# Linear attention with a soft mixture of experts on one core: the log magnitudes as two F32R parts, the key and query factors in one product, the turns found on ScalarE, and a new order of issue

## The chip, the core and the metric

The kernel runs on one core of a Trainium2 chip. The metric is the device time of one execution in microseconds, as the median of several runs. The engines are TensorE (PE, with its weight loads PEld), VectorE (DVE), ScalarE (ACT), GpSimd (POOL) and SyncE (SP), which issues all transfers here.

## The reference

Two parts follow each other. The first is a gated linear attention with complex decay, for 4 batches, 8 heads, 768 tokens and 48 channels:

```
scale = min(|a|, 0.999) / (|a| + 1e-6);  a = a * scale          # a = a_re + i a_im
for t in tokens:
    S = a[t][:, None] * S;  S.re += k[t] v[t]^T                 # 48 x 48 per head
    y[t] = q[t] . S.re
```

The second takes y as x of 3072 tokens by 384 channels and applies a soft mixture of 8 experts with 4 slots each: logits x @ phi, a softmax over all tokens that forms the 32 slots, two matrix products with a relu per expert, and a softmax over the slots that mixes their outputs into each token.

## The kernel before, in words

The tokens are cut into 24 blocks of 128 (six of each batch, g = 0 to 23), and three blocks make a unit u of 0 to 7. Tokens lie on the partitions; the 8 x 48 = 384 channels lie along a row. Instead of stepping through the tokens, each block is worked in polar form, with these steps (each a generator whose pieces are issued one at a time):

- `gates` (g in the order table; whole units, the first unit in two groups of 1 and 2 blocks): on ScalarE and VectorE, from the two parts of a, the tangent of the angle in `aat[:, 1]` and twice the log magnitude in `aat[:, 0]`. L642, L644, L646, L652 and L656 are on ScalarE; L648, L650, L654 and L658 on VectorE.
- `arctan` (t): the angle, L665 on ScalarE.
- `phase` (p, per block): L676 sums the angles along the tokens by a triangular product (`up`, in turns, since the triangle holds 1/2pi). VectorE rounds to whole turns by adding and subtracting a large constant (L679, tile `n`) and subtracts (L681, tile `f`); ScalarE takes sine (L686) and cosine (L691) into `cs`. L673 adds the block before's last turn to this block's first row.
- `expo` (e, per block): L702 sums the log magnitudes by another triangular product (`lp`, F32); L706 and L708 take its exponent with both signs into `ee`. One row of it goes to memory and comes back as the block's total decay (L711, L715).
- `mults` (m, per block): L723 multiplies `ee` with queries and keys; L732 then forms, for queries and for keys, the product with `cs`: two products of 768 columns into `hat0` and `hat1`. Block 0 does its part in two pieces (L728).
- `xpose` (x): four transposes per half of the heads and per side (L744, `tp`), copied by ScalarE (L747, `hT`).
- `score` (c): L752 (`sp`), masked by VectorE (L756, `scT`).
- `attend` (a): L777 and L779 into `yb`, copied by ScalarE as `yT` (L782).
- `delta` (D): the state's update, L790 (`db`), L795, L797 (`st`).
- `xform` (f), `logits` (l), `slots` (s), `shares` (q): the output turned back (`xp`, `xs`) and the running softmax sums of the experts' slots (`lg`, `mt`, `sip`, `lt`, `lct`).

After block 23 come `merge`, the experts (`hidden`, `turn`, `experts`) and the mixing (`combine0`, `combine1`) with the stores. Exponent and logarithm are in one table of ScalarE, sine and arctangent in another; L577 and L580 load them in turn, about once each per unit. `warm` (wu) issues a product whose result nobody reads.

What sets the order of the work is a long text, `ORDER`. Each name in it issues the next piece of that step, and `_InOrder` ties each instruction to the one before it on its engine. So the engines work in the order of this text, each at its own pace, and a wait holds up all that stands behind it on the same engine. The loads (la, lq, lv, w) are names in the same text and go to SP's queue.

Of the kernel before, what the change touches and what calls it, by code (L numbers as in the profile page):

```python
# [86 lines left out]
class _Moe:  # L87
# [227 lines left out]
    wu3 c5 g3 T2 p3 p3 p3 e4 a1 m4 p5 p5 m3 c4 la2 c5 D2 D2 a2 t3 m3 x14 x14 p4 m3 p5 p4 p4 p6 g3 p5 p5 x12 x12 a2 a2 p5 e5 g4
    D2 D3 D3 m4 m4 x16 x16 x15 x15 p6 D2 p6 x18 m5 p7 x13 x13 l0 p7 L3 x18 m5 m5 l0 p7 D3 g4 g4 f1 f1 x17 p8 x17 c6 e7 e7 e7 f2
    g4 c6 c7 f2 e6 e6 e6 x23 x23 x19 g4 g4 lq1 p8 e8 a3 c7 a3 l0 s0 e8 p8 g4 d1 q0 q0 e8 x20 w0 x19 x20 g4 D3 a3 T3 p6 p6 p8 c8
    c8 p8 g4 x21 x21 c9 c9 D4 D4 D4 x22 e6 x22 m6 p7 p7 a4 a4 D4 c10 c11 lv1 m6 x26 t4 p7 p9 m6 p9 c10 p8 p9 a4 x25 x24 s0 D5 D5
    e7 m7 e8 L4 a5 c11 a5 x25 x24 c12 x26 p10 m7 la3 g5 x28 m7 q0 s0 q0 p10 f3 c12 x27 a5 g5 d2 D5 a6 q0 g5 x28 D6 f3 p10 q0 g5
    x30 x30 x27 m8 g5 m8 x29 e9 e9 m8 e9 x31 x31 e10 e10 e9 l1 l1 e10 g5 c13 c13 x29 x34 x34 e11 c14 e11 lq2 e11 g5 p11 g5 c14  # L320
    q1 f4 f4 q1 q1 T4 D6 D6 x33 x35 x35 x32 x32 g5 p11 a6 a6 p11 p11 p9 p9 p9 c15 c15 s0 s0 s0 x33 p11 e10 m10 a7 a7 p10 c17 m9
    p10 t5 c16 a7 p11 D6 lv2 D7 D7 m9 x36 p10 q1 q1 p12 c16 la4 a8 c17 a8 g6 L5 e11 g6 g6 x38 x38 q1 e13 m9 p12 a8 x39 x39 lv3
    e12 D7 D8 D8 x36 e12 e12 x37 m10 x42 p13 m10 x37 g6 w1 l1 s1 x40 c18 x40 g6 x42 c19 D7 g6 x43 x41 e13 e13 d3 c18 a9 c19 a9
    a9 x41 m11 D8 D9 x43 m11 m11 e12 e14 e14 e14 g6 g6 f7 p13 p13 p14 x47 x47 lq3 m12 f7 T5 c21 c21 p12 c20 D9 p12 c20 p12 x45
    t6 x46 x46 x45 s1 p14 D8 f5 f5 x44 p14 x44 a10 a10 s1 l2 la5 p15 p15 m12 x50 D9 x50 e13 m12 p13 p13 p13 c22 e14 g6 x49 x48
    x49 x48 p14 p14 c22 p14 D10 D10 a10 l2 q2 c23 p15 D9 d4 p15 p16 p16 g7 p15 p15 q2 c23 x51 x51 m13 m13 f6 s1 f6 a11 a11 a11
# [756 lines left out]
```

## Time and profile before

| | |
|---|---|
| median of the runs shown | 300.86 us (299.57 to 302.11, 3 runs) |
| the profiled execution | 302.44 us |
| its span, first to last instruction | 300.6 us |
| busy: PE, PEld, DVE, ACT, POOL | 271.5, 214.2, 236.5, 213.5, 2.8 us |
| chain that ended last, by engine | PE 65%, DMA 12%, ACT 11%, DVE 7% |
| mean granted TensorE clock | 0.960 |

A row of the groups reads: line, engine, operation, output from inputs, shape and count, then the busy time in us and the mean of one in ns, then the idle time of that engine just before and what ended it. F32 products show two records each. In the rows of stretches the columns are the length, the busy time (and count) of PE, PEld, DVE, ACT and POOL, the granted TensorE clock (1.00 is full), the transfers' share and their rate. A row in order of time gives the start, the time taken and what was done; in brackets stands the idle time before it.

### The profile page before, as it was taken

What the parts mean: (1) busy time and instruction counts of PE and PEld (TensorE: products, weight loads), DVE (VectorE), ACT (ScalarE), POOL (GpSimd) and SP (SyncE); (2) the same over time, 40 slices, a digit from 0 to 9 for tenths busy, and PEclk for the clock granted to TensorE, in tenths of its full rate; (3) what the DMA queues carried; (4) which work ended last, traced back from release to release, by engine and by line L of the source; (5) the groups of instructions that cost most, each with busy time, mean ns of one, the idle gap of its engine ahead of it and who ended that gap; (6) DMA issues with size and microseconds to landing.
All of it is one profiled execution on the core that took longest, in us unless ns stands there. A gap on an engine that the chain in (4) does not pass through costs nothing.

```text
span 300.6 us, 6641 instructions
## 1 busy us (share of the span) xinstructions
PE 271.5 (90%) x2694; PEld 214.2 (71%) x2694; DVE 236.5 (79%) x453; ACT 213.5 (71%) x377; POOL 2.8 (1%) x7
## 2 busy tenths in 40 slices
PE   0649599989999999899999999999999999999990
PEld 0135488778888877888878887888898997336760
DVE  1468789899999999999998999998979565714350
...
GB/s 244 422 219 3 75 86 3 98 313 48 142 98 2 80 295 89 186 126 160 3 15 302 354 375 11 14 190 240 218 19 266 148 423 256 241 342 423 184 384 200
DMA packets 20788, 54.85 MB, mean 182 GB/s; under 512 B 11536, under 2 KB 13456, under 8 KB 16144
## 3 DMA queue, kind: packets, MB, share of 16 engines
...
q8 instruction: 23, 0.38, 0.6%
q14 instruction: 13, 0.11, 0.1%
...
## 4 chain that ended last, share of the span: by engine, by line
PE 65%; DMA 12%; ACT 11%; DVE 7%; issue 2%; SPq 0%; DVEq 0%; ACTq 0%
PE sp L752 12%; PE tp L744 11%; DMA aat<-in_aa_dram 8%; PE yb L777 6%; PE db L790 5%; DMA rows<-ee 5%; PE lp L702 4%; PE yb L779 4%; PE up L676 4%; PE hp L229 3%; PE op L259 3%; PE xp L802 3%; PE lg L109 2%; PE ep L277 2%; ACT gt L642 2%
## 5 line engine op out<-in xcount | busy, mean ns | idle before, releaser
L747 ACT COPY hT<-tp 96x512 f32<-96x512 f32 x96 | 53.5, 583 | 17.9 <-PE tp L744 17.8
L744 PE MATMUL tp<-cst,hat 128*96 128x128 f32 x384 | 57.2, 287 | 4.0 <-DVE hat L732 3.8
L744 PEld LDWEIGHTS tp<-cst,hat 128*96 128x96 f32 x384 | 45.0, 134 | 13.5 <-issue 5.8
L752 PE MATMUL sp<-hT,hT 96*128 96x128 f32 x384 | 51.6, 282 | 0.9 <-ACT hT L747 0.9
L752 PEld LDWEIGHTS sp<-hT,hT 96*128 96x128 f32 x384 | 47.2, 194 | 5.3 <-issue 2.5
L732 DVE TENSOR_TENSOR hat<-ee,cs 128x768 f32<-128x768 f32 x48 | 44.6, 951 | 2.3 <-PE tp L744 0.9
L777 PE MATMUL yb<-scT,vt 128*48 128x128 f32 x384 | 37.2, 280 | 3.5 <-DVE scT L756 3.5
L756 DVE TENSOR_TENSOR scT<-sp,cst 128x512 f32<-128x512 f32 x48 | 32.6, 684 | 3.7 <-PE sp L752 3.5
L790 PEld LDWEIGHTS db<-vt,hat 128*96 128x96 f32 x320 | 30.2, 165 | 4.2 <-issue 1.7
L790 PE MATMUL db<-vt,hat 128*96 128x48 f32 x320 | 30.8, 246 | 1.3 <-DVE st L795 1.3
L779 PE MATMUL yb<-hT,st 96*48 96x128 f32 x320 | 31.2, 272 | 0.0
L777 PEld LDWEIGHTS yb<-scT,vt 128*48 128x48 f32 x384 | 21.2, 123 | 11.2 <-issue 3.9
L723 DVE TENSOR_TENSOR ee<-ee,qkt 128x768 f32<-128x768 f32 x23 | 21.8, 951 | 4.8 <-DMA rows<-ee 3.3
L676 PE MATMUL up<-aat,cst 128*128 128x384 f32 x48 | 21.5, 532 | 3.2 <-ACT aat L665 2.9
L702 PE MATMUL lp<-aat,cst 128*128 128x384 f32 x48 | 21.5, 531 | 0.9 <-DVE aat L658 0.5
L779 PEld LDWEIGHTS yb<-hT,st 96*48 96x48 f32 x320 | 19.2, 123 | 0.0
L782 ACT COPY yT<-yb 128x512 f32<-128x512 f32 x24 | 14.0, 582 | 6.5 <-PE yb L779 6.5
L648 DVE TENSOR_TENSOR aat<-aat,gt 128x1152 f32<-128x1152 f32 (+2 forms) x9 | 11.0, 1219 | 8.8 <-ACT gt L646 8.8
L805 ACT COPY xs<-xp 128x384 f32<-128x384 f32 x24 | 11.3, 476 | 8.6 <-PE xp L802 8.6
L679 DVE TENSOR_SCALAR n<-up 128x384 f32<-128x384 f32 x24 | 13.2, 550 | 2.6 <-PE up L676 2.5
L802 PE MATMUL xp<-cst,yT 128*128 128x128 f32 x96 | 14.4, 274 | 0.4 <-DVE scT L756 0.4
L706 ACT ACTIVATE ee<-lp 128x384 f32<-128x384 f32 x24 | 11.8, 492 | 4.2 <-PE lp L702 4.0
...
## 6 DMA issues: line engine op xcount, KB each, us to landing
...
```

Source lines behind the costliest of these rows:

```text
L676: PE.matmul(out=up, lhsT=tri_u[par], rhs=ph, start=True, stop=True)
L702: PE.matmul(out=lp, lhsT=tri_l[par], rhs=aat[u][:, 0, j], start=True, stop=True)
L723: DVE.tensor_tensor(out=e, in0=e, in1=qkt[u][:, j], op=ALU.mult)
L732: DVE.tensor_tensor(out=x, in0=e[:, w].rearrange("p (h d) -> p h d", d=D).unsqueeze(2).broadcast_to([P, H, 2, D]), in1=cs[g], op=ALU.mult,)
L744: PE.transpose(out=tp[:, a, :], in_=hat[g][w][:, 4 * hh + a].rearrange("p c d -> p (c d)"), identity=ident)
L747: ACT.copy(out=hT[g, hh, w], in_=tp)
L752: PE.matmul(out=sp[:, a, :], lhsT=hT[g, hh, 1][:, a, :], rhs=hT[g, hh, 0][:, a, :], start=True, stop=True)
L756: DVE.tensor_tensor(out=t, in0=sp, in1=mask[g % 2].unsqueeze(1).broadcast_to([P, 4, P]), op=ALU.mult)
L777: PE.matmul(out=o, lhsT=vt[u][:, j, h, :], rhs=scT[g, hh][:, a, :], start=True, stop=first)
L779: PE.matmul(out=o, lhsT=st[g - 1][:, h, :], rhs=hT[g, hh, 0][:, a, :], start=False, stop=True)
L790: PE.matmul(out=db[:, h, :], lhsT=hat[g][1][:, h].rearrange("p c d -> p (c d)"), rhs=vt[u][:, j, h, :], start=True, stop=True)
L802: PE.transpose(out=xp[:, c].rearrange("p a d -> p (a d)"), in_=yT[g][:, c, :], identity=ident)
```

## The change

Five edits, and the order text written anew.

- `gates` ends with two more pieces: ScalarE copies the log magnitude into an F32R tile (its first part), and VectorE subtracts that from the full value into a second F32R tile. `expo` makes two F32R products of these in place of the F32 one, with F32R copies of the triangles (`tri_t`, one VectorE copy at the start).
- `phase` rounds on ScalarE: the large constant is the bias of a copy of `up`. VectorE subtracts constant and `up` in one instruction, which turns the sign of `f`; the scales of its users are turned too.
- `mults` makes one product of 1536 columns for queries and keys together, in a tile with two buffers (before, one of 768 for queries and two for keys). Block 0 is handled like the others.
- Fourteen warming products in place of four. They read a tile that GpSimd sets to zero, and so wait for no transfer.
- The scratch for dynamic transfers is set to 1024.

```diff
-BUF = dict(wx=7, wt=2, f=3, cs=4, ee=3, hat0=1, hat1=2, hT0=4, hT1=3, scT=2, st=2, xs=5, yT=5, we=4)
+BUF = dict(wx=7, wt=2, f=3, cs=4, ee=3, hat=2, hT0=4, hT1=3, scT=2, st=2, xs=5, yT=5, we=4)
 ORDER = """
-    i0 L0 g0 g0 g0 i6 i1 wu2 wu1 g0 g0 g0 g0 i3 g0 g0 i4 i2 g1 g1 e0 i8 g1 g1 la0 i7 e0 e0 wu0 lv0 T0 t0 g1 t1 e0 p0 p0 p0 p0 p0
+    wu13 wu2 L0 i0 g0 g0 wu12 g0 g0 i4 i3 i2 g1 wu6 g0 g0 wu9 i1 i5 g0 wu0 g1 tr0 g0 g0 g0 wu4 g0 g1 e0 wu10 e0 e0 wu8 T0 t0 g1
...
-    tri_l = [cst[:, C_TL : C_TL + P], cst[:, C_TL + P : C_MK]]
+    tri_t = cp.tile([P, 2 * P], F32R, name="tri_t")
+    tri_r = [tri_t[:, 0:P], tri_t[:, P : 2 * P]]
...
         DVE.scalar_tensor_tensor(out=ar, in0=ar, scalar=W_MAX, in1=t, op0=ALU.min, op1=ALU.subtract)
+        yield "g9"
+        if u not in parts:
+            parts[u] = [eo.tile([P, UB, HD], F32R, name=f"w{x}", bufs=1) for x in range(2)]
+        hi, lo = (w[:, j0:j1] for w in parts[u])
+        ACT.activation(out=hi, in_=ar, func=AF.Copy)
+        yield "g10"
+        DVE.tensor_tensor(out=lo, in0=ar, in1=hi.bitcast(F32), op=ALU.subtract)
...
-        DVE.tensor_scalar(out=n, in0=up, scalar1=MAGIC, scalar2=MAGIC, op0=ALU.add, op1=ALU.subtract)
+        ACT.activation(out=n, in_=up, func=AF.Identity, bias=kb[:, 4:5])
+        yield "p2b"
...
-        DVE.tensor_tensor(out=f, in0=up, in1=n, op=ALU.subtract)
+        DVE.scalar_tensor_tensor(out=f, in0=n, scalar=MAGIC, in1=up, op0=ALU.subtract, op1=ALU.subtract)
...
-        PE.matmul(out=lp, lhsT=tri_l[par], rhs=aat[u][:, 0, j], start=True, stop=True)
+        for x in range(2):
+            PE.matmul(out=lp, lhsT=tri_r[par], rhs=parts[u][x][:, j], start=x == 0, stop=x == 1)
...
-        for w in range(2):
-            if g == 0:
-                yield f"n{w}"
-                DVE.tensor_tensor(out=e[:, w], in0=e[:, w], in1=qkt[u][:, j, w], op=ALU.mult)
-            yield f"m{w}"
-            x = wk.tile([P, H, 2, D], F32, name=f"hat{w}", bufs=BUF[f"hat{w}"])
-            hat[g].append(x)
...
+        x = wk.tile([P, 2, H, 2, D], F32, name="hat", bufs=BUF["hat"])
+        hat[g] = [x[:, w] for w in range(2)]
+        sh = [P, 2, H, 2, D]
+        DVE.tensor_tensor(
+            out=x,
+            in0=e.rearrange("p w (h d) -> p w h d", d=D).unsqueeze(3).broadcast_to(sh),
+            in1=cs[g].unsqueeze(1).broadcast_to(sh),
+            op=ALU.mult,
+        )
...
+    blank = cp.tile([P, P], F32, name="blank")
+    POOL.memset(blank, 0.0)
...
-        PE.matmul(out=wp, lhsT=ident, rhs=cst[:, 0:512], start=True, stop=True)
-    for x in range(4):
+        PE.matmul(out=wp.rearrange("p (a c) -> p a c", a=4), lhsT=blank, rhs=blank.unsqueeze(1).broadcast_to([P, 4, P]), start=True, stop=True)
+    for x in range(14):
...
+    at("tr", lambda: DVE.tensor_copy(out=tri_t, in_=cst[:, C_TL:C_MK]) and None)
...
-    nc = _bacc.Bacc("TRN2", target_bir_lowering=False, num_devices=1)
+    nc = _bacc.Bacc("TRN2", target_bir_lowering=False, num_devices=1, dynamic_dma_scratch_size=1024)
```

Three places show what the new order text does. First TensorE's queue at the start, before (`wp` is a warming product, `hat` a block's factors):

```order
L904 MATMUL wp<-cst 128x512 x2
L702 MATMUL lp<-aat,cst 128x384
L904 MATMUL wp<-cst 128x512
L676 MATMUL up<-aat,cst 128x384
L744 MATMUL tp<-cst,hat_170 96x128 x8
```

and now:

```order
L913 MATMUL wp<-blank 128x512 x7
L713 MATMUL lp<-w_149,tri_t 128x384
L713 MATMUL lp<-w_150,tri_t 128x384
L913 MATMUL wp<-blank 128x512 x2
L685 MATMUL up<-aat,cst 128x384
L913 MATMUL wp<-blank 128x512
L685 MATMUL up<-aat,cst 128x384
L750 MATMUL tp<-cst,hat 96x128 x4
```

Seven warming products now stand ahead of the first `lp` pair, two between it and the first `up`, and the second block's `up` comes ahead of the first transposes. `w_149` is the first part, `w_150` the second.

Next ScalarE's queue at the start, before:

```order
L646 ACTIVATE gt<-aat 128x384
L652 ACTIVATE gt<-gt,kb 128x384
L656 ACTIVATE gt<-aat,kb 128x384
L642 ACTIVATE gt,amiss<-aat,kb 128x768
L644 ACTIVATE aat<-aat 128x768
L646 ACTIVATE gt<-aat 128x768
L706 ACTIVATE ee<-lp 128x384
```

and now:

```order
L648 ACTIVATE gt<-aat 128x384
L644 ACTIVATE gt,amiss<-aat,kb 128x768
L654 ACTIVATE gt<-gt,kb 128x384
L646 ACTIVATE aat<-aat 128x768
L658 ACTIVATE gt<-aat,kb 128x384
L665 ACTIVATE w_149<-aat 128x384
L648 ACTIVATE gt<-aat 128x768
L717 ACTIVATE ee<-lp 128x384
```

The passes of 768 columns (blocks 1 and 2) are now woven between those of block 0, and the first part (L665) stands ahead of the third of them.

Last SP's queue at the start, before:

```order
L617 DMA aat<-in_aa_dram 128x2x384
L596 DMA vt<-in_vv_dram 128x1152
L617 DMA cst<-in_consts_dram 128x640
L617 DMA aat<-in_aa_dram 128x2x384 x2
L617 DMA qkt<-in_qk_dram 128x768
```

and now:

```order
L619 DMA aat<-in_aa_dram 128x2x384 x3
L619 DMA qkt<-in_qk_dram 128x768
L619 DMA cst<-in_consts_dram 128x640
L619 DMA cst<-in_consts_dram 128x741
L590 DMA aat<-in_aa_dram 128x2304
```

All three blocks of `aat` come first; the constants, which the warming products no longer read, come after them and after the first queries and keys.

More of the change, by code (lines that the diff above doesn't have):

```diff
@@ L315 @@
[L315 to L326, printed above, removed]
@@ new lines @@
+    p5 p5 x13 x15 x15 g3 x10 la2 x10 p6 p6 p6 a1 x12 g3 p5 p5 p5 L3 c5 c5 D2 a2 a2 a2 p7 p7 p7 m5 g4 x12 g4 x14 x14 g4 D3 g3 D3
+    f0 f0 m4 p7 l0 l0 m5 l0 e6 e6 e6 x16 x16 lv1 c6 c6 d1 g4 f2 g4 f2 e7 e7 e7 e8 e8 e8 x17 x17 c7 c7 x21 x21 p8 g4 lq1 q0 D3 q0
+    q0 s0 D3 x20 x20 g4 x19 x19 p8 D4 p8 a3 a3 g4 x18 x18 T3 x22 w1 D4 e6 m6 e7 p8 p6 p6 p6 lq2 a3 la3 c8 q0 q0 x22 x23 g4 g4 c8
+    x23 t4 c10 p8 p8 p8 a4 p7 p7 c9 p7 m6 x24 D4 e8 x27 x27 g5 m7 d2 c9 x24 D5 D5 D4 m8 q0 p9 c10 s0 s0 a4 a4 p9 p9 f1 m7 f1 c11
@@ new lines @@
+    c11 x25 x25 L4 a5 a5 g5 x26 x26 c12 g5 p9 g4 e9 e9 e9 p10 f3 e9 f3 c13 a5 m8 c12 x31 g5 e10 e10 e10 c13 x29 g5 p10 p10 x31
+    p10 p11 D5 f4 f4 g5 g5 e11 e11 x34 w2 e11 a6 a6 x28 l1 l1 a6 x29 D6 g5 m9 q1 q1 g5 l1 x28 q1 x32 s0 x34 q1 x30 x30 x32 p11
+    p11 T4 s0 s0 c14 p9 p9 p9 x35 x35 p11 D6 D6 x33 c15 c14 a7 c17 p11 p11 t5 p12 g5 e10 c15 a7 q1 p11 p12 m9 x38 x33 c16 la4 D6
+    x39 g6 D7 D7 a7 g5 e11 m11 lq3 p12 p10 c16 c17 a8 a8 p10 x38 x39 c19 x37 p10 e13 q1 L5 g6 g6 p13 d3 m10 e12 e12 s1 D7 x37
@@ new lines @@
+    x49 x48 x48 c25 c25 c24 c24 a11 e15 g7 e15 e15 e16 e16 g7 x52 x52 m14 D11 D11 D11 x55 x55 lv4 g7 g7 x54 x54 D11 e16 p17 p17
+    p17 x53 x53 x56 q2 x56 q2 c27 g7 g7 l3 l3 a12 a12 a12 e17 e17 e17 lq5 c27 c26 c26 g7 T6 f8 t7 f8 D12 s2 x58 x58 x59 x59 s2
+    a13 a13 m15 m15 p17 g7 x57 x57 q2 q2 p18 e16 m16 p18 p16 p18 p19 D12 a13 f10 f10 q3 e17 c29 p18 D12 g7 f9 p16 p17 p16 c29
+    c28 c28 x61 p19 p17 q3 p19 f9 L7 x60 g7 d5 s2 D13 D13 D12 x60 q3 x62 x62 a14 a14 s2 m16 x61 p19 la6 g8 x67 e18 e18 e18 s2
@@ L569, in _polar @@
     DVE.memset(kb[:, 3:4], AR_MIN)
+    DVE.memset(kb[:, 4:5], MAGIC)
     W_MAX = 2.0 * math.log(MAG_CAP)
@@ L598, in load_first @@
     def load_first(x):
-        if x == 0:
+        if x in (0, 3, 4) and 0 not in aat:
             aat[0] = io.tile([P, 2, UB, HD], F32, name="aat")
-        if x == 2:
+        if x in (2, 7) and 0 not in qkt:
             qkt[0] = io.tile([P, UB, 2, HD], F32, name="qkt")
@@ L632, in wload @@
             SP.dma_start(out=t[:, 0:c], in_=w2[x - NW1][:, 0:c])
-    tmp = {}
+    tmp, parts = {}, {}
     def gates(x):
@@ L672, in phase @@
         if g % NBLK:
-            DVE.scalar_tensor_tensor(out=ph[r], in0=fr[g - 1][r], scalar=2.0 * math.pi, in1=ph[r], op0=ALU.mult, op1=ALU.add)
+            DVE.scalar_tensor_tensor(out=ph[r], in0=fr[g - 1][r], scalar=-2.0 * math.pi, in1=ph[r], op0=ALU.mult, op1=ALU.add)
             yield "p1"
@@ L685, in phase @@
         cs[g] = t
-        ACT.activation(out=t[:, :, 1, :], in_=f.rearrange("p (h d) -> p h d", d=D), func=AF.Sin, scale=TWO_PI)
+        ACT.activation(out=t[:, :, 1, :], in_=f.rearrange("p (h d) -> p h d", d=D), func=AF.Sin, scale=-TWO_PI)
         yield "p4"
@@ L721, in mults @@
         e = ee[g]
[L722 to L737 removed]
+        DVE.tensor_tensor(out=e, in0=e, in1=qkt[u][:, j], op=ALU.mult)
+        yield "m0"
+        x = wk.tile([P, 2, H, 2, D], F32, name="hat", bufs=BUF["hat"])
[7 more added lines that the diff above has]
+        )
     hT, scT = {}, {}
```

57 lines of the change are left out of this document (24 added, 33 removed).

## Prediction

> **What bounds the kernel now.** I read the busy rows of four stretches first, cut at the copies of yT (L782) of blocks 0, 12 and 23 (48.34, 157.69 and 249.82 us), then the groups by line and shape, the chain of waits, and the order of time in the first 50 us.
>
> ```profile
> core 0: us, PE busy (x) PEld busy (x) DVE busy (x) ACT busy (x) POOL busy (x), PEclk, DMA share, GB/s
> 48.34:157.69 109.35, 106.72 (x1060) 89.67 (x1059) 104.70 (x183) 95.83 (x168) 0.00 (x0) 0.98 0.42 113
> 157.69:249.82 92.13, 91.11 (x999) 79.57 (x1000) 78.18 (x155) 64.99 (x123) 0.14 (x1) 1.00 0.62 211
> 0.00:48.34 48.34, 30.73 (x144) 20.45 (x144) 31.83 (x52) 37.51 (x56) 0.20 (x4) 0.82 0.55 163
> 249.82:300.60 50.78, 42.89 (x500) 24.52 (x498) 21.79 (x67) 15.19 (x34) 2.44 (x3) 0.97 0.75 297
> ```
>
> The four stretches have different limits. Up to block 0's output no engine is full: it is a chain of short steps between ScalarE, VectorE and TensorE. From block 0 to block 12, TensorE is busy 98% and VectorE 96%, while ScalarE has 109.35 - 95.83 = 13.5 us free. From block 12 to 23, TensorE alone is full (99%; VectorE 85%, ScalarE 71%). The tail belongs to the experts, which the change leaves alone. So a microsecond of TensorE is worth its full price from block 12 on; before that it is worth it only if the two other engines let TensorE use it.
>
> **The log-magnitude products.** These rows carry the price: one F32 product (two records) in the chain, the F32R products of the tail, and a few others that I need below.
>
> ```profile
> 97.65 0.65 PE lp L702 x2
> 290.31 3.28 PE o L298 x24
> 130.10 0.65 PE up L676 x2
> 198.45 0.88 PE tp L744 x8
> 204.72 0.89 PE sp L752 x8
> 231.72 1.32 PE db L790 x16
> 211.09 1.00 PE lg L109 x24
> ```
>
> An F32 product of 384 columns costs 0.65 us. An F32R product of 256 columns costs 3.28 / 24 = 0.137 us, weight load included. A column of one pass is 0.65 / (4 x 384) = 0.42 ns if F32 makes four passes, which fits: 256 columns are 0.11 of the 0.137. So 384 columns are 0.137 + 128 x 0.00042 = 0.19, and the pair 0.38 us, an estimate from these rows. The bounds are 0.28 (two rows of 256 columns, too short) and 0.65 (no cheaper at all). Each block saves 0.65 - 0.38 = 0.27 us of TensorE, 5.7 us over the 21 blocks whose products run after 48 us. FP8 and Floating Point Precision of the Trainium skill (TensorE Precision Notes) has four passes for true FP32 against a reduced form that truncates; by that the pair would be half of 0.65, 0.33, and the sum 1.1 us better. The row of the tail, with its weight loads, is the dearer one and I keep it.
>
> **VectorE.** It loses n, gains the second part of the magnitude, and does one product where it did two.
>
> ```profile
> L732 DVE TENSOR_TENSOR hat<-ee,cs 128x768 f32<-128x768 f32 x48 | 44.6, 951 | 2.3 <-PE tp L744 0.9 <-PE db L790 0.9
> L728 DVE TENSOR_TENSOR ee<-ee,qkt 128x384 f32<-128x384 f32 x2 | 1.1, 555 | 0.5 <-DMA rows<-ee 0.5
> L679 DVE TENSOR_SCALAR n<-up 128x384 f32<-128x384 f32 x24 | 13.2, 550 | 2.6 <-PE up L676 2.5
> L658 DVE SCALAR_TENSOR_TENSOR aat<-aat,gt 128x1152 f32<-128x1152 f32 x7 | 9.4, 1349 | 0.0
> L178 DVE SCALAR_TENSOR_TENSOR acc<-acc,al,sip 96x384 f32<-96x384 f32 x7 | 4.2, 606 | 2.4 <-PE sip L173 2.2
> L681 DVE TENSOR_TENSOR f<-up,n 128x384 f32<-128x384 f32 x24 | 13.4, 558 | 0.8
> ```
>
> 384 more columns cost 951 - 555 = 396 ns, so one product of 1536 columns is 951 + 2 x 396 = 1743 ns, against 1902 for two: 0.16 a block, 3.8 in all. n goes: 24 x 0.55 = 13.2. The second part is a pass of L658's shape: 7 x 1.35, and 0.95 + 0.56 for the two short groups of the start, 11.0 back. f turns into the form of L178, up to 0.05 dearer a block (1.2), and the cast of tri_t is below 0.6 by the 384-column row. In all VectorE gets about 4.5 us lighter. The first transposes of a block now wait for both halves of hat, 1743 instead of 951 ns; in the full stretches TensorE has other blocks' work queued ahead, without which this would cost 0.8 a block.
>
> **ScalarE.** It gets n (24) and the first part (nine).
>
> ```profile
> L706 ACT ACTIVATE ee<-lp 128x384 f32<-128x384 f32 x24 | 11.8, 492 | 4.2 <-PE lp L702 4.0
> L644 ACT ACTIVATE aat<-aat 128x1152 f32<-128x1152 f32 x7 | 8.2, 1165 | 0.1
> L644 ACT ACTIVATE aat<-aat 128x768 f32<-128x768 f32 x1 | 0.8, 843 | 0.0
> L644 ACT ACTIVATE aat<-aat 128x384 f32<-128x384 f32 x1 | 0.5, 522 | 0.0
> L805 ACT COPY xs<-xp 128x384 f32<-128x384 f32 x24 | 11.3, 476 | 8.6 <-PE xp L802 8.6
> L652 ACT ACTIVATE gt<-gt,kb 128x1152 f32<-128x1152 f32 x7 | 8.9, 1271 | 0.4 <-DVE tmax L650 0.4
> 26.03 1.16 ACT L646 ACTIVATE gt<-aat 128x1152 f32<-128x1152 f32 x1
> 27.10 0.47 ACT L706 ACTIVATE ee<-lp 128x384 f32<-128x384 f32 x1
> 27.47 0.48 ACT L708 ACTIVATE ee<-lp 128x384 f32<-128x384 f32 x1
> ```
>
> n has the shape of L706 (492 ns; 0.37 from start to start, 27.10 to 27.47, when queued back to back), the first part that of L644 (1165 ns; 1.07, 26.03 to 27.10). Counted in the new order, block 0 to 12 gains 14 n, 4 first parts and one L652 and loses one xs (0.48): 6.9 + 4.7 + 1.3 - 0.5 = 12.4 us by durations, about 10.4 by starts. ScalarE would then be busy 106.2 of 109.35 us. All of its slack goes.
>
> **The sum, by stretches.** *To block 0.* ScalarE gains four n and first parts of 384, 768 and 1152 columns: 1.97 + 0.52 + 0.84 + 1.17 = 4.5 us.
>
> ```profile
> 7.90 0.61 ACT L652 ACTIVATE gt<-gt,kb 128x384 f32<-128x384 f32 x1 [1.23 <-DVE tmax L650]
> 9.14 0.61 ACT L656 ACTIVATE gt<-aat,kb 128x384 f32<-128x384 f32 x1 [0.63 <-DVE aat L654]
> 38.67 0.58 ACT L747 COPY hT<-tp 96x512 f32<-96x512 f32 x1 [0.38 <-PE tp L744]
> 40.38 1.07 ACT L747 COPY hT<-tp 96x512 f32<-96x512 f32 x2 [1.12 <-PE tp L744]
> 41.95 0.58 ACT L747 COPY hT<-tp 96x512 f32<-96x512 f32 x1 [0.50 <-PE tp L744]
> ```
>
> The granted clock in the same stretch (the column before the last two):
>
> ```profile
> 0.00:17.30 17.30, 6.13 (x10) 2.17 (x10) 6.02 (x16) 10.27 (x17) 0.20 (x4) 1.00 0.91 318
> 17.30:27.50 10.20, 7.25 (x19) 3.92 (x20) 7.51 (x12) 9.11 (x13) 0.00 (x0) 0.50 0.32 114
> 34.40:41.10 6.70, 6.42 (x30) 5.51 (x31) 6.60 (x8) 5.17 (x7) 0.00 (x0) 0.50 0.48 150
> ```
>
> The two gaps near 8 us (1.86) get block 1 and 2's passes, as the order shows; the three near 40 (2.0) are waits for transposes at the half clock. Together 3.9 of the 4.5 is covered: I take 0 for this stretch, with +4.5 if nothing is hidden and -2 if the transposes near 40 us run at full clock.
>
> The warming products must not hold up the first lp.
>
> ```profile
> 6.97 3.71 PE L904 MATMUL wp<-cst 128*128 128x512 f32 x4 [6.97 <-DMA cst<-in_consts_dram]
> 10.52 0.82 PE L702 MATMUL lp<-aat,cst 128*128 128x384 f32 x2
> 11.17 1.02 PE L904 MATMUL wp<-cst 128*128 128x512 f32 x2
> ```
>
> That lp started at 10.52 and now comes some 0.5 later (one ScalarE pass more). Two products took 3.71 us at first, one 1.02 later. Seven of them, starting near 1 us, take 13 us if all run like the first and hold lp to 14 (+3, inside the bound above); with two slow and five at 0.87 (0.65 x 512/384) they end near 9 and hold nothing. I take the second. TensorE: Matmul & The Clock Gate of the Trainium skill (What's actually happening) says that the array starts at half clock and is released after about 3.4 us of activity; the 3.71 agrees, though the clock row above prints 1.00 there.
>
> *Block 0 to 12.* The new order also moves work into this stretch: TensorE gets 14 pairs for 13 products (14 x 0.38 - 13 x 0.65 = -3.1), one up more (+0.65), 12 transposes (+1.3), 4 scores (+0.9), 8 db (+1.3), one lg group (+1.0), and loses a warming product (-0.9): +1.2 us. VectorE loses about 6 here (14 n and two hats leave, five second parts come). With ScalarE's slack down from 13.5 to 3 us, some of TensorE's supply (hT, cs, ee) must come late: I add 1.8, bounds 0 and 7, the upper end being most of the 12.4 less the 2.6 us that TensorE is idle now and the 3 that are left. Sum +3.
>
> *Block 12 to 23.* Here the work that moved is missing: lp -2.5 (7 pairs for 8 products), up -0.65, transposes -1.3, scores -0.9, db -1.3, lg -1.0: -7.7 us. ScalarE gains 4 and VectorE loses about 3, so both stay under 83% of the 84 us left, and the gain is kept; at worst 3 us of it is lost to waits.
>
> Total 0 + 3 - 7.7 = -4.7 us; the tail 0. The profiled execution took 302.44 us with a span of 300.6, so this gives 297.7. The median of the runs is 1.58 lower, 300.86, and the forecast in its terms 296.2 us.
>
> **Rivals.**
>
> *ScalarE takes over.* Place: from the start to block 12. The 4.5 and 12.4 us land on the path as they are: +16.9 - 7.7 = +9.2, 310.1 us. It decides as soon as 7.7 of the 16.9 is not hidden, and makes the kernel slower by 1% from 10.7 on. For it: ScalarE would be at 97%, in order, between two engines above 90%. Against it: VectorE ran at 96% beside a TensorE of 98%.
>
> *It is eaten up.* The wait in the middle is 6.5 instead of 1.8 us, near its upper bound: 300.9 us, no change. For it: three engines above 90% share one order and short buffers. Against it: TensorE waited only 2.6 us there with two such engines.
>
> *The pair is no cheaper*: 14 x 0.27 + 7 x 0.27 = 5.7 lost, 301.9 us, no change. The 0.137 of the tail speaks against it.
>
> *The clock stays up.* TensorE ran at half clock from 17.3 to 27.5 and from 34.4 to 41.1 us. At full clock the 7.25 and 6.42 us of work there would be half, 6.8 us less; if 2 of that is on the path besides the 2 us of gaps at 40 us, the start gains 4 and the time is 292.2. For it: the warming products fill TensorE's gaps before 30 us. Against it: they end by about 35, and a product at half clock costs double. By the same page and section an idle window of 3.4 us throttles again; the drop at 17.3 after a stretch with 0.9 us of work agrees.
>
> **How the numbers follow.** Forecast 0.50, with its own range 293 to 299; clock 0.13 (292); eaten up 0.17 (301); pair no cheaper 0.07 (302); ScalarE 0.13 (303 to 310). A measurement here tells about 1%, 3 us, from no change. Faster: 0.47 of the forecast and the clock, 0.60; slower 0.12, since a little of the ScalarE case stays within 1%; same 0.28. The range is 291 to 303: it takes in the clock case and the eaten-up case and leaves most of the ScalarE case out.
>
> **What would show it.** Right: lp pairs near 0.4 us in the chain; hat near 1.74 us; ScalarE above 95% and TensorE above 96% between the copies of blocks 0 and 12, that stretch 110 to 115 us long; block 12 to 23 near 84.5 us; the first copy of yT between 46 and 50 us. Wrong: TensorE idle before tp or sp for more than 8 us in the middle, with ScalarE as what ended it; or a last stretch as long as before.

## The result, and the profile after

The changed kernel takes 297.19 us (median of 4 runs, 296.47 to 298.75) against 301.06 of the kernel before (4 runs): ratio 0.9885, with an interval of 0.9848 to 0.9921. So it is faster by 1.15%, 3.9 us; the forecast was 296.2, range 291 to 303. The profiled execution took 298.75 us, the slowest of the four, its span 296.9. Here and below a median is of all runs of a kernel, while ratio and interval leave out the slow runs, those more than 1.5% above its fastest.

The same four stretches as before, cut at the copies of yT (now L788) of blocks 0, 12 and 23; the columns are those of the rows of before:

```profile
core 0: us, PE busy (x) PEld busy (x) DVE busy (x) ACT busy (x) POOL busy (x), PEclk, DMA share, GB/s
50.45:158.78 108.33, 105.00 (x1103) 91.50 (x1102) 104.76 (x168) 105.98 (x186) 0.00 (x0) 1.00 0.52 147
158.78:246.48 87.70, 86.70 (x968) 78.13 (x971) 74.35 (x135) 67.65 (x128) 1.81 (x1) 1.00 0.52 175
0.00:50.45 50.45, 36.98 (x150) 20.83 (x151) 32.11 (x47) 40.62 (x63) 0.41 (x5) 0.90 0.49 157
246.48:296.90 50.42, 42.13 (x500) 24.26 (x499) 21.91 (x67) 15.96 (x37) 0.78 (x2) 0.96 0.78 311
```

Read the lengths against those of before: start +2.1, middle -1.0, late stretch -4.4, tail -0.4. Then the busy times of TensorE, VectorE and ScalarE in the middle: 105.0, 104.8 and 106.0 of 108.3 us. Three engines are at 97 or 98% at once, ScalarE up from 88%. The late stretch is TensorE's as before (99%).

The groups that answer to the prediction's:

```profile
L738 DVE TENSOR_TENSOR hat<-ee,cs 128x1536 f32<-128x1536 f32 x24 | 42.0, 1751 | 1.3 <-ACT cs L701 0.7
L688 ACT ACTIVATE n<-up,kb 128x384 f32<-128x384 f32 x24 | 14.2, 590 | 2.4 <-PE up L685 2.4
L701 ACT ACTIVATE cs<-n,kb 128x384 f32<-128x384 f32 x24 | 14.6, 615 | 0.9 <-DVE n L699 0.9
L696 ACT ACTIVATE cs<-f 128x384 f32<-128x384 f32 x24 | 12.6, 527 | 0.7 <-DVE f L691 0.6
```

The product of 1536 columns takes 1751 ns and n on ScalarE 590. The last two rows differ in their operand kb: the form that reads a bias (615) is 0.09 us longer than the one without (527), and n reads one.

In the order of time, one F32R pair and the product behind it:

```profile
126.71 0.60 PE L713 MATMUL lp<-w,tri_t 128*128 128x384 f32 x2
127.15 0.81 PE L685 MATMUL up<-aat,cst 128*128 128x384 f32 x2
```

The next product starts 0.44 us after the pair did, where the F32 product took 0.65. Two pairs in a row took 0.80 (121.60 to 122.40 us).

The chain that ended last, by engine and by line:

```profile
PE 61%; DMA 17%; ACT 10%; DVE 7%; issue 1%; SPq 1%; DVEq 0%; ACTq 0%
DMA rows<-ee 10%; PE sp L758 10%; PE tp L750 9%; PE yb L783 6%; PE db L796 5%; DMA rt<-rows 5%; PE yb L785 4%; PE op L259 4%; PE up L685 4%; PE hp L229 4%; PE xp L808 3%; PE lp L713 2%; DMA aat<-in_aa_dram 2%; PE lg L109 2%; PE ep L277 2%; PE sip L173 2%
```

The share of the transfers has grown (17% against 12%), by the small ones of the decays: rows has 10% where it had 5%, and rt 5%. Whether they cost what the share says is tried below.

### The profile page after: what moved, and what is told of

Read it like the earlier page. It is cut to its first block, busy times and chain, and to the rows that moved or that the text cites. A ratio compares the mean times of both kernels' runs of the same rounds, so it can differ in the third digit from the quotient of the medians.

```text
span 296.9 us, 6662 instructions
## 1 busy us (share of the span) xinstructions
PE 270.8 (91%) x2714; PEld 214.7 (72%) x2714; DVE 233.1 (79%) x415; ACT 230.2 (78%) x410; POOL 3.0 (1%) x8
## 4 chain that ended last, share of the span: by engine, by line
PE 61%; DMA 17%; ACT 10%; DVE 7%; issue 1%; SPq 1%; DVEq 0%; ACTq 0%
DMA rows<-ee 10%; PE sp L758 10%; PE tp L750 9%; PE yb L783 6%; PE db L796 5%; DMA rt<-rows 5%; PE yb L785 4%; PE op L259 4%; PE up L685 4%; PE hp L229 4%; PE xp L808 3%; PE lp L713 2%; DMA aat<-in_aa_dram 2%; PE lg L109 2%; PE ep L277 2%; PE sip L173 2%
## 5 line engine op out<-in xcount | busy, mean ns | idle before, releaser
L750 PE MATMUL tp<-cst,hat 128*96 128x128 f32 x384 | 55.3, 277 | 3.7 <-DVE hat L738 3.7
L750 PEld LDWEIGHTS tp<-cst,hat 128*96 128x96 f32 x384 | 42.7, 128 | 12.0 <-issue 3.8
L738 DVE TENSOR_TENSOR hat<-ee,cs 128x1536 f32<-128x1536 f32 x24 | 42.0, 1751 | 1.3 <-ACT cs L701 0.7
L733 DVE TENSOR_TENSOR ee<-ee,qkt 128x768 f32<-128x768 f32 x24 | 22.8, 952 | 3.7 <-DMA rows<-ee 3.4
L788 ACT COPY yT<-yb 128x512 f32<-128x512 f32 x24 | 14.1, 589 | 10.3 <-PE yb L785 9.8
L913 PE MATMUL wp<-blank 128*128 128x512 f32 x28 | 18.6, 800 | 1.0 <-POOL blank L908 1.0
L713 PE MATMUL lp<-w,tri_t 128*128 128x384 f32 x48 | 14.9, 392 | 4.2 <-ACT w L665 2.5
L691 DVE SCALAR_TENSOR_TENSOR f<-n,up 128x384 f32<-128x384 f32 x24 | 13.1, 546 | 4.2 <-ACT n L688 4.2
L688 ACT ACTIVATE n<-up,kb 128x384 f32<-128x384 f32 x24 | 14.2, 590 | 2.4 <-PE up L685 2.4
L701 ACT ACTIVATE cs<-n,kb 128x384 f32<-128x384 f32 x24 | 14.6, 615 | 0.9 <-DVE n L699 0.9
## 6 DMA issues: line engine op xcount, KB each, us to landing
wx<-in_w_dram SPq DMA_DIRECT2D x5, 1152.0 KB, 10.3
```

The costliest lines, as they stand in the source:

```text
L713: PE.matmul(out=lp, lhsT=tri_r[par], rhs=parts[u][x][:, j], start=x == 0, stop=x == 1)
L733: DVE.tensor_tensor(out=e, in0=e, in1=qkt[u][:, j], op=ALU.mult)
L738: DVE.tensor_tensor(out=x, in0=e.rearrange("p w (h d) -> p w h d", d=D).unsqueeze(3).broadcast_to(sh), in1=cs[g].unsqueeze(1).broadcast_to ...
L750: PE.transpose(out=tp[:, a, :], in_=hat[g][w][:, 4 * hh + a].rearrange("p c d -> p (c d)"), identity=ident)
L913: PE.matmul(out=wp.rearrange("p (a c) -> p a c", a=4), lhsT=blank, rhs=blank.unsqueeze(1).broadcast_to([P, 4, P]), start=True, stop=True)
```

## The experiments

My account after the result was this: the middle is held by three engines together, the late stretch by TensorE, and the gain needs the new order and the edits at once. The rivals were that the order alone did it, that the F32R pair alone did it, and that ScalarE is the new bound. Times are medians, ratios are to the kernel before in the same series with their 95% intervals. The changed kernel stands at 0.9885 (0.9848 to 0.9921).

### The new order with the old work

```diff
-        ACT.activation(out=n, in_=up, func=AF.Identity, bias=kb[:, 4:5])
+        DVE.tensor_scalar(out=n, in0=up, scalar1=MAGIC, scalar2=None, op0=ALU.add)
...
-        for x in range(2):
-            PE.matmul(out=lp, lhsT=tri_r[par], rhs=parts[u][x][:, j], start=x == 0, stop=x == 1)
+        PE.matmul(out=lp, lhsT=tri_l[par], rhs=aat[u][:, 0, j], start=True, stop=True)
...
+        for w in range(2):
+            DVE.tensor_tensor(
+                out=x[:, w],
```

> The changed kernel's order of issue and its 14 warming products, with the old work in them: one F32 lp product per block, n rounded on VectorE, two hat products of 768 columns per block, no first and second parts. Nothing of the computation is left out. Account by stretches (mine): in the changed kernel TensorE, VectorE and ScalarE were busy 105.0, 104.8 and 106.0 of the 108.3 us between the yT copies of blocks 0 and 12. With the old work TensorE gets about 0.21 us per block back (3 in the middle, 2 to 2.5 in the late stretch), VectorE gets 14 n and the split hats back in the middle (+7) and needs over 110 us: 301.5 to 303 us, that is 4 to 6 over the changed kernel. Rival, the order and the warming products did it: 297. Rival, the order alone costs and only the edits gain: 305 or more.

Measured: 309.69 us, 1.0297 (1.0255 to 1.0340). That is 12.5 us over the changed kernel where I expected 4 to 6, and where the second rival had 305 us or more. Its middle and late stretch:

```profile
49.32:164.78 115.46, 109.51 (x1106) 92.17 (x1105) 107.00 (x186) 97.32 (x167) 0.00 (x0) 1.00 0.46 139
164.78:255.89 91.11, 89.30 (x968) 78.22 (x971) 75.77 (x150) 63.16 (x119) 1.81 (x1) 1.00 0.48 166
```

The middle is 7.1 us longer than in the changed kernel, and no engine is full in it: TensorE 95%, VectorE 93%. The order alone gains nothing; with the old work it is worse than the old order.

### The old order with the new edits, and the same with the turns back on VectorE

```diff
 ORDER = """
-    wu13 wu2 L0 i0 g0 g0 wu12 g0 g0 i4 i3 i2 g1 wu6 g0 g0 wu9 i1 i5 g0 wu0 g1 tr0 g0 g0 g0 wu4 g0 g1 e0 wu10 e0 e0 wu8 T0 t0 g1
+    i0 L0 g0 g0 g0 i6 i1 wu2 wu1 g0 g0 g0 g0 i3 g0 g0 g0 i4 i2 g1 g1 tr0 g0 e0 i8 g1 g1 la0 i7 e0 e0 wu0
...
```

n and f stand together where the old text had both; the second parts stand ahead of their unit's first lp.

> The order text of the kernel before, with only the names that the edits need put in, and all the edits (F32R pair, turns on ScalarE, one hat product); four warming products from the blank tile. Nothing of the computation is left out. Account by stretches: the saving of the pair (0.21 us per block, 5 in all) is there, but ScalarE's 16.7 us stand in an order that was not made for them, and one hat product of 1.75 us ahead of the transposes comes where two shorter ones let TensorE start earlier: TensorE waits more, 301 to 305 us. Rival, the edits alone did it: 297 or less.

Measured: 351.53 us, 1.1699 (1.1644 to 1.1754), far beyond what any theory gave. The waits say where (engine, output and line, what it waited for, us in total, times, longest):

```profile
DVE f L696 <- ACT n L693: 47.8, 21, 4.1
```

```profile
PE lp L718 <- DVE w L672: 16.1, 5, 6.1
PE tp L755 <- DVE hat L743: 12.6, 10, 4.4
PE lp L718 <- ACT w L670: 9.1, 3, 5.8
```

VectorE has up's rounding right ahead of f in the old text. With n on ScalarE it stands still there until TensorE's product has gone through ScalarE's queue, some 2.3 us a block. TensorE stands still for parts that are made too late and for the whole of hat. Its clock is lower too: granted 0.91 in the middle, where the changed kernel has 1.00. To part the first wait from the others, n went back:

```diff
-        ACT.activation(out=n, in_=up, func=AF.Identity, bias=kb[:, 4:5])
+        DVE.tensor_scalar(out=n, in0=up, scalar1=MAGIC, scalar2=None, op0=ALU.add)
```

> The kernel with the old order and all the edits (351.53 us) with the turns taken back to VectorE, all else as there. Nothing of the computation is left out. In that run VectorE waited 47.8 us in 21 places for n, since f stands right behind it in the old order, and lp 25 us for the parts. My theory: the round trip through ScalarE is most of the loss; with n on VectorE it is gone and 13 us of VectorE work come back: 315 to 328. Rival, the late parts are the loss, and the wait for n lies beside it: 340 or more. Rival, it goes back to the kernel before: 300 to 305.

Measured: 332.75 us, 1.1056 (1.1005 to 1.1108): between my theory (up to 328) and the first rival (340 or more). The wait for n is gone and takes 19 us with it, even though VectorE has 13 us more to do; the other waits of TensorE are as they were:

```profile
PE lp L718 <- DVE w L672: 18.5, 7, 5.9
PE tp L755 <- DVE hat L743: 12.3, 10, 4.4
PE lp L718 <- ACT w L670: 9.4, 4, 6.1
```

So the round trip of n is a good third of the loss of 50 us. The rest (31 us) goes with waits for the late parts and the undivided hat and with a clock of 0.96 in the middle, which I did not part from each other.

### The changed kernel with one edit undone

First the turns:

```diff
-        ACT.activation(out=n, in_=up, func=AF.Identity, bias=kb[:, 4:5])
+        DVE.tensor_scalar(out=n, in0=up, scalar1=MAGIC, scalar2=None, op0=ALU.add)
```

> The changed kernel with n rounded on VectorE, at the same place of the order. Nothing of the computation is left out. ScalarE loses 24 x 0.59 = 14.2 us, VectorE gains 24 x about 0.55 = 13. Account by stretches: in the middle VectorE has 104.8 + 7.7 = 112.5 us of work in a stretch of 108.3, so this grows by 4 to 6: 301 to 303 us. Rival, ScalarE is the bound since the change: 293 to 295, since it is then idle 10 us there. Rival, TensorE alone is the bound: 297.

Measured: 310.27 us, 1.0314 (1.0271 to 1.0356). This one edit is worth 13 us in the new order, over three times the gain of the whole change. ScalarE as the only bound is out: it has 4.4 us less to do in the middle, and that stretch is longer. The middle stretch (the late one is 90.33 us), and then the waits of TensorE and of VectorE in the middle:

```profile
49.31:167.98 118.67, 108.74 (x1105) 93.35 (x1103) 110.69 (x177) 101.59 (x171) 0.00 (x0) 0.99 0.46 135
```

```profile
PE yb L783 <- DVE scT L762: 2.3, 4, 1.1
PE lp L713 <- DVE f L691: 1.8, 1, 1.8
PE tp L750 <- DVE hat L738: 1.8, 2, 1.1
```

```profile
DVE n L688 <- PE up L685: 5.2, 4, 2.0
DVE scT L762 <- PE sp L758: 1.3, 1, 1.3
```

VectorE's 110.7 us no longer fit into 108.3, which explains 2.4 of the 10.3 us. The rest is in the pairs of lines: TensorE waits for VectorE's scT, f and hat, VectorE waits for TensorE's up and sp. I take it that each is late because the other was, and that this is why the stretch is longer than the work of its busiest engine.

Next the F32R pair:

```diff
-        for x in range(2):
-            PE.matmul(out=lp, lhsT=tri_r[par], rhs=parts[u][x][:, j], start=x == 0, stop=x == 1)
+        PE.matmul(out=lp, lhsT=tri_l[par], rhs=aat[u][:, 0, j], start=True, stop=True)
```

> The changed kernel with the F32 lp product in place of the pair of F32R products, and without the first and second parts. Nothing of the computation is left out. Account by stretches: TensorE gets 0.21 us per block back, ScalarE loses the first parts (9.3 us in all, 4.7 in the middle) and VectorE the second parts (about 10 in all). Late stretch, TensorE alone at its limit: +1.5 to +2. Middle, three engines near their limit: TensorE +2.9 and the others less, so +0 to +1.5. Start, without three passes: -1. Sum about +1.5, 298 to 300 us. Rival, the pair did it all (TensorE the only bound): +5, 302. Rival, ScalarE is the bound: -4, 293.

Measured: 297.66 us, 0.9893 (0.9849 to 0.9937): no difference from the changed kernel that these runs can tell. The middle and the late stretch; the first number is block 0's copy, so the start took 47.30 us:

```profile
47.30:156.73 109.43, 108.37 (x1106) 92.19 (x1105) 100.55 (x162) 102.44 (x181) 0.00 (x0) 1.00 0.51 147
156.73:245.39 88.66, 88.66 (x968) 78.37 (x971) 71.70 (x133) 65.76 (x125) 1.81 (x1) 1.00 0.49 169
```

The pair does save TensorE's time: 108.37 - 105.00 = 3.4 us in the middle, which holds 25 records or 12.5 pairs, and 2.0 over six to seven pairs in the late stretch, so 0.27 to 0.30 a block. But of the 3.4 us the middle gets only 1.1 (109.43 to 108.33): TensorE's idle time there goes from 1.1 to 3.3 us, while ScalarE and VectorE, with the parts, have 106.0 and 104.8 instead of 102.4 and 100.6 us to do. And the start is 3.1 us shorter here. The parts that stood ahead of lp are one reason for that and chance is another, as the kernels on the start show.

Last, two products of 768 columns for hat, in the same tile:

```diff
-        DVE.tensor_tensor(
-            out=x,
...
+        for w in range(2):
+            DVE.tensor_tensor(
+                out=x[:, w],
```

> The changed kernel with two products of 768 columns in the hat tile in place of one of 1536, issued together in the same place. Nothing of the computation is left out. VectorE gains 24 x (2 x 0.951 - 1.751) = 3.6 us by durations, 2.1 of it in the middle, where it was busy 104.8 of 108.3 us. Since the n on VectorE (+13 us of VectorE work) cost 13 us of time, VectorE's work in the middle goes through nearly one to one: 299 to 301. Rival, VectorE only matters once it is the longest of the three: 297 to 298. Rival, the first half is ready earlier for the transposes, which gains: 296.

Measured: 297.17 us, 0.9883 (0.9841 to 0.9924). The single product is worth nothing that can be seen. The middle:

```profile
50.56:158.25 107.69, 105.25 (x1104) 91.64 (x1104) 105.26 (x180) 105.90 (x185) 0.00 (x0) 1.00 0.51 148
```

VectorE's 105.3 us still fit (the late stretch is 86.72 us). My expectation added the durations of two products. But queued back to back the two take 1.82 us (from 124.95 us on) where one takes 1.75, so VectorE got 0.5 us more to do in the middle and not 2.1. That is too little to tell whether its work goes through "one to one".

### The turns and the order without pair and single hat

The two edits above together.

> The changed kernel's order and warming products with the turns on ScalarE and nothing else of the change: F32 lp product without parts, and two hat products of 768 columns. Nothing of the computation is left out. So far the F32 product in it took 297.66 and the two hat products 297.17, each no different from the changed kernel's 297.19, while the turns back on VectorE took 310.27 and all the old work in the new order 309.69. My theory: the gain is that of the turns on ScalarE together with an order made for it, and pair and single hat product add nothing: 297 to 298.5. Rival, pair and hat product stand in for each other, and one of them is needed: 300 or more.

Measured: 301.19 us beside 301.86 of the kernel before, 0.9966 (0.9934 to 0.9997). So my theory fails: each of the two may be left out, but not both without loss; they are worth about 0.8% together, 2.4 us. The middle and late stretch:

```profile
50.91:160.81 109.90, 108.18 (x1106) 92.19 (x1105) 101.36 (x174) 102.45 (x182) 0.00 (x0) 1.00 0.50 145
160.81:249.84 89.03, 89.03 (x968) 78.44 (x971) 72.25 (x142) 65.86 (x125) 1.81 (x1) 1.00 0.49 169
```

This kernel and the one with two hat products differ by the pair alone. Their intervals lie apart (0.9934 to 0.9997 against 0.9841 to 0.9924), and the middle and late stretch are 2.2 and 2.3 us longer without the pair. So beside two hat products the pair is worth 0.8%, 2.5 us. Read as steps, the ratios are 1.0297 for the new order (with its warming products) and the old work, 0.9966 with the turns on ScalarE, 0.9883 with the pair and 0.9885 with the single hat product. Behind the first, each of these steps is one edit. The intervals lie apart up to the pair; the last step is worth nothing that can be seen.

Beside the single hat product, undoing the pair cost nothing that could be told. Both stretches here are within 0.5 us of that F32 kernel's. What differs most from it in the profiles is the start, 50.91 against 47.30 us. With the intervals (the F32 kernel's and this one's still touch) I read it so: the pair gives 1 to 2 us there too, which a lucky start had hidden. That reading is not shown; it may also be the two hat products that lengthen the start (see below).

### The start: first unit in F32, and no warming products

```diff
+        if u == 0:
+            return
         yield "g9"
...
+        if u == 0:
+            PE.matmul(out=lp, lhsT=tri_l[par], rhs=aat[u][:, 0, j], start=True, stop=True)
+        else:
+            for x in range(2):
...
```

> The changed kernel with the F32 lp product and no parts for unit 0 alone (blocks 0 to 2); the pair from unit 1 on. Nothing of the computation is left out. With the F32 product everywhere the time was 297.66, as good as the changed kernel, and the stretches told two effects that cancel: the start 3.15 us shorter (47.30 against 50.45), the rest 1.1 and 1.0 us longer. My theory: the parts cost where they stand ahead of the first lp of block 0 and of the blocks 1 and 2, and pay elsewhere; so this kernel has the short start (47 to 48) and nearly the short middle and late stretches (108.5 and 87.7): 294 to 295.5. Rival, the shorter start was chance (the second load of aat landed 1.15 us earlier in that profile) or is given back in a middle that all three engines bound: 297.

Measured: 296.39 us, 0.9843 (0.9804 to 0.9882); middle and late stretch 108.78 and 87.17 us as expected, but block 0's copy only at 50.40. This profile is of the slowest of its six runs (298.30 us), so the others may have a shorter start. Why it did not get shorter in this one, TensorE's order of time tells. The changed kernel, the first seven warming products having ended at 9.9 us:

```profile
12.26 0.44 PE L713 MATMUL lp<-w,tri_t 128*128 128x384 f32 x1 [2.35 <-ACT w L665]
12.85 0.45 PE L713 MATMUL lp<-w,tri_t 128*128 128x384 f32 x1 [0.15 <-DVE w L667]
13.14 3.56 PE L913 MATMUL wp<-blank 128*128 128x512 f32 x4
16.50 0.86 PE L685 MATMUL up<-aat,cst 128*128 128x384 f32 x2
```

```profile
12.00:16.00 4.00, 3.58 (x6) 1.42 (x6) 2.48 (x4) 3.59 (x7) 0.00 (x0) 0.65 0.25 55
```

With the F32 product everywhere:

```profile
10.56 0.91 PE L704 MATMUL lp<-aat,cst 128*128 128x384 f32 x2 [0.28 <-DVE aat L659]
11.31 1.88 PE L904 MATMUL wp<-blank 128*128 128x512 f32 x4
14.25 0.91 PE L677 MATMUL up<-aat,cst 128*128 128x384 f32 x2 [1.07 <-ACT aat L666]
```

```profile
12.00:16.00 4.00, 2.93 (x7) 0.87 (x5) 0.82 (x3) 3.50 (x5) 0.00 (x0) 1.00 0.35 23
```

And with only the first unit in F32:

```profile
12.02 1.65 PE L716 MATMUL lp<-aat,cst 128*128 128x384 f32 x2 [2.90 <-DVE aat L661]
13.46 2.65 PE L919 MATMUL wp<-blank 128*128 128x512 f32 x4
16.45 0.91 PE L688 MATMUL up<-aat,cst 128*128 128x384 f32 x2 [0.34 <-ACT aat L677]
```

After an idle time of 2.35 or 2.90 us the granted clock falls (0.65 from 12 to 16 us in the changed kernel) and the same two warming products take 3.56 or 2.65 us instead of 1.88, ahead of the first up; after 0.28 us it stays at 1.00.

Two things set that idle time. One is the load of blocks 1 and 2's aat, for which ScalarE waited until 8.29, 7.14 and 8.60 us in these three executions: its passes stand between block 0's, so block 0 waits with it. The order wove them, as ScalarE's queue of the change shows. From there to the first lp it is 3.97 us in the changed kernel and 3.42 in the two others. So the parts cost 0.55 us at this place, and the load varies by up to 1.5. The other is the end of the first seven warming products, at 9.9, 10.3 and 9.1 us.

Not all of the start is decided there. From the first db to block 0's copy it is 23.9 us with the F32 product everywhere, 24.7 in the two others, and 26.5 and 26.9 in the kernels with two hat products and the turns on ScalarE. Whether the hat products or chance make this difference was not tried. In two kernels whose start is the same, the changed one and the one with the decays first (below), block 0's copy comes at 50.45 and 48.70. Such differences hide what the parts cost.

Without any warming product (all fourteen wu out of the order):

```diff
-    wu13 wu2 L0 i0 g0 g0 wu12 g0 g0 i4 i3 i2 g1 wu6 g0 g0 wu9 i1 i5 g0 wu0 g1 tr0 g0 g0 g0 wu4 g0 g1 e0 wu10 e0 e0 wu8 T0 t0 g1
+    L0 i0 g0 g0 g0 g0 i4 i3 i2 g1 g0 g0 i1 i5 g0 g1 tr0 g0 g0 g0 g0 g1 e0 e0 e0 T0 t0 g1
```

> The changed kernel without any warming product. Nothing of the computation is left out. My theory: the first products then run at half clock, and TensorE's gaps before 30 us bring the granted clock down for longer (the kernel before, with four, ran at 0.50 from 17.3 to 27.5 and from 34.4 to 41.1 us); start +2 to +3, so 299 to 300. Rival, they only stand in TensorE's queue ahead of lp and up (two of them at 1.8 us each ahead of the first up): -1, 296. Rival, nothing of it is on the path: 297.

Measured: 299.27 us, 0.9929 (0.9894 to 0.9963). By the medians that is 2 us slower than the changed kernel, as my theory had it, by the ratios 1.3. The intervals overlap, so the loss is likely and not shown.

### Transfers that stand in the chain

The change's queue of SyncE around the last unit's decays, in order of time:

```profile
214.65 6.16 SPq L631 DMA_DIRECT2D wx<-in_w_dram  x3
220.90 0.59 SPq L631 DMA_DIRECT2D aat<-in_w_dram  x1
221.60 0.60 SPq L631 DMA_DIRECT2D qkt<-in_w_dram  x1
222.29 1.24 SPq L726 DMA_DIRECT2D rt<-rows  x2
```

```profile
222.90 15.01 DMA rt<-rows
```

The last row is from the chain in order of time: rt takes 15.01 us, and VectorE waits 2.5 us for it. The edit:

```diff
-    x82 a19 q5 c40 c40 p22 p22 x83 e23 D16 s4 x83 x84 lv6 p23 p23 x85 x84 p23 w4 w5 x86 x86 s4 x85 c41 c41 x87 a20 a20 p22 m22
...
-    w7 w8 x89 x89 m23 a21 a21 a21 x93 x93 q5 q5 f18 f18 q6 q6 q5 d7 D18 D19 D19 x92 x92 x90 x90 x94 s5 c44 c44 x95 x94 c45 f20
+    e23 D16 s4 x83 x84 lv6 p23 p23 x85 x84 p23 d7 w4 w5 x86 x86 s4 x85 c41 c41 x87 a20 a20 p22 m22 m22 D17 s4 a20 p23 p23 x87
```

> The changed kernel with the load of the last unit's decays (rt of unit 7) moved ahead of the five large weight loads that stand before it in SP's queue. Nothing of the computation is left out. In the changed kernel it is issued at 222.3 us and takes 15 us, which stands in the chain of waits with 5%. My theory: TensorE, the bound there, was idle only 1.0 us between 224 and 246 us, so what the wait costs is at most 1 us: 296 to 297. Rival, the chain is right and the wait is on the path: 292 to 295.

Measured: 296.63 us, 0.9863 (0.9828 to 0.9899), no difference that can be told from the changed kernel. Its late stretch:

```profile
156.46:243.09 86.63, 86.63 (x968) 78.13 (x971) 74.44 (x135) 67.66 (x127) 1.81 (x1) 1.00 0.50 169
```

TensorE is never idle, and the stretch is 1.07 us shorter than in the changed kernel's profile; the kernel with two hat products had 86.72 without this edit. So the 5% of the chain (15 us) were worth 1 us at most, the idle time of the engine that bounds the stretch.

Three edits together: first unit in F32, decays first, and unit 1's aat (la0) and the rest of the constants (i5) loaded after what block 0 needs:

```diff
-    g1 t1 p0 p0 la0 p0 p0 p0 e0 m0 wu3 p1 p0 m0 L1 g1 g1 p1 p1 i7 g1 g1 x2 p1 x2 wu1 i6 p2 D0 wu11 g2 g1 g1 i8 g2 e1 lv0 g2 g2
+    T0 t0 g1 g1 t1 p0 p0 p0 p0 p0 e0 la0 m0 wu3 p1 p0 m0 L1 g1 g1 p1 p1 i7 i5 g1 g1 x2 p1 x2 wu1 i6 p2
```

> The changed kernel with three edits together: F32 lp for unit 0 alone (alone 296.39), the last unit's decays ahead of the weight loads (alone 296.63), and the load of unit 1's aat and of the rest of the constants behind the pieces that block 0 needs. Nothing of the computation is left out. The second load of aat held ScalarE until 7.1 to 9.6 us in the runs so far, and what follows to block 0's yT copy took 40.2 to 42.5 us whatever that was; with 2.5 MB less ahead of it it should come by 7 us: start -1. Sum of the three 0.8 + 0.6 + 1: 294 to 295.5. Rival, the start is not on the path of the whole (given back in the middle): 296 to 297.

Measured: 297.32 us beside 301.86, 0.9853 (0.9815 to 0.9891): near the rival's number, but not for its reason, since the start did not get shorter. The load held ScalarE until 7.55 us only (the two loads moved are 1.5 MB together, not the 2.5 of my expectation) and the clock stayed at 1.00 from 8 to 16 us, but block 0's copy came at 50.62. Another load is late in its place; the first db tells which (in the changed kernel it waited for no load):

```profile
25.59 0.88 PE L806 MATMUL db<-vt,hat 128*96 128x48 f32 x8 [1.88 <-DMA vt<-in_vv_dram]
```

The last kernel also moves one of the two warming products behind lp ahead of it:

```diff
-... wu4 g0 g1 e0 wu10 e0 e0 wu8 ...
+... wu4 g0 g1 wu10 e0 e0 e0 wu8 ...
```

> As the kernel with the three edits together, and one of the two warming products between the first lp and the first up moved ahead of lp. Nothing of the computation is left out. In the changed kernel the first seven end at 9.9 us, TensorE is idle until 12.3, the granted clock then falls to half and the two warming products behind lp take 3.56 us and hold up the first up to 16.50; with the F32 product, which came 0.28 us behind the warming products, the clock stayed at 1.00 there. My theory: without the gap the clock stays up and the first up comes some 0.5 earlier: 0.3 to 1 us less than the kernel with the three edits. Rival, the next gap (3 us ahead of the second up) brings the clock down anyway, a little later: the same time.

Measured: 298.81 us beside 301.86, 0.9885 (0.9846 to 0.9925). Not faster, which is the rival. By the ratios it is 1 us slower than the kernel before it, but the intervals overlap:

```profile
11.01 1.02 PE L923 MATMUL wp<-blank 128*128 128x512 f32 x2
13.96 1.23 PE L692 MATMUL up<-aat,cst 128*128 128x384 f32 x2 [1.93 <-ACT aat L681]
```

```profile
16.00:20.00 4.00, 2.10 (x4) 0.50 (x2) 3.53 (x5) 3.25 (x4) 0.00 (x0) 0.50 0.88 361
```

The gap has only moved: 1.93 us ahead of up, and the clock is at 0.50 from 16 to 20 us. No kernel of these is shown to beat the changed one; the best interval (0.9804 to 0.9882) overlaps its own. The scratch size and the handling of block 0 were not tried by themselves.

## Why the prediction was right, and where it was not

**The sum** was -4.7 us, measured -3.7 between the two profiles (-3.9 by medians). Its terms were 0, +3, -7.7 and 0; measured +2.1, -1.0, -4.4 and -0.4. Middle and late stretch miss by 4.0 and 3.3 us with opposite signs: the step that failed is the work that the order moves from one to the other. I priced what leaves the late stretch, the products lp apart, at 5.2 us and took it as added to the middle. The F32 kernel has the new order and the old product: TensorE's busy time in its late stretch is 88.66, against 91.11 before, so all that moved is 2.5 us. The records of the late stretch tell what stayed, first before, then after:

```profile
L744 PE MATMUL tp<-cst,hat 128*96 128x128 f32 x156 | 21.7, 274 | 0.2
L790 PE MATMUL db<-vt,hat 128*96 128x48 f32 x136 | 13.2, 246 | 0.0
```

```profile
L750 PE MATMUL tp<-cst,hat 128*96 128x128 f32 x156 | 22.5, 274 | 0.0
L796 PE MATMUL db<-vt,hat 128*96 128x48 f32 x128 | 12.1, 245 | 0.0
```

The 12 transposes of my list did not move, and of the 16 records of db half did. Up stayed (12 records), the scores nearly (172 to 168), and four xp came in (44 to 48). Only lg went as listed (96 to 72). There were seven lp products to replace and not eight (14 records).

The total was spared, since what is wrongly moved from one stretch to the other drops out of it. In both together TensorE's busy time fell by 6.1 us (1.7 and 4.4), where the forecast had 6.5. The waits that I added in the middle, 1.8 us, were 0.7 (idle time 2.6 to 3.3). The start's +2.1 was made up for by the smaller waits and by the tail (-0.4); that is luck. Of the signs named beforehand, those of the lp pair, of hat and of the two busy shares held. The lengths of the middle (110 to 115 us, measured 108.3) and of the late stretch (84.5, measured 87.7) and the place of the first copy (46 to 50, measured 50.45) did not.

**The pair** was right as a size: 0.27 us a block forecast, 0.27 to 0.30 measured in busy time. By start to start it is 0.44, dearer than my 0.38, and two in a row take 0.80. An estimate from FP8 and Floating Point Precision of the Trainium skill (TensorE Precision Notes) was 0.33; the trace is dearer. As a cause it was overrated: undoing it alone left the time where it was, and beside two hat products it was worth 2.5 us of the 5.7 that I had for it.

**VectorE** is the step with no term in the sum. I worked out that n (13.2 us) goes and 11.0 come back for the second parts, and let it rest at "about 4.5 us lighter" (measured 236.5 to 233.1). In the middle I had it losing about 6 us, and it went from 104.7 to 104.8: n took 7.7 us out and the larger hat product 0.8, but four second parts brought 5.4, and the order moved some 4 us in (two scT, two updates of st, one f, one pass of gates). So it stayed as full as it was. That n moved is what lets the new order run at all: with n on VectorE it takes 310.27. My argument that VectorE at 96% beside a full TensorE had cost nothing before was true of the old order. With the old work the new order has TensorE and VectorE busy for 109.5 and 107.0 us in the middle, against 106.7 and 104.7.

**ScalarE**: 106.2 of the middle's time forecast, 106.0 measured; above 95% as named. n was mis-sized (492 forecast, 590 measured), since the row that I took it from has no bias. The rival that ScalarE takes over stayed away: in the two kernels where it has less to do the middle is longer (109.4 and 118.7 us), though in each of them another engine has more to do.

**The start** was taken at 0 with bounds -2 and +4.5; measured +2.1, and 48.70 instead of 50.45 in the kernel whose start is the same. "Hold nothing" was wrong for the warming products: the first seven end at 9.9, near the 9 forecast, but two more stand at half clock ahead of the first up. Here gaps of 1.9 to 2.9 us were enough to bring the clock down: in the changed kernel TensorE had 0.90 us of work from 9.8 to 13.2 us, and from 13.2 to 16.6 the clock was 0.50. By TensorE: Matmul & The Clock Gate of the Trainium skill (What's actually happening) an idle window of about 3.4 us throttles; the traces show it with a shorter gap.

**The late stretch**: I did not see that the new order puts the last decays behind five weight loads. It cost 1.0 us at most, which is all the idle time of TensorE there, as much as before.
